# Two attentions on one core: the order of units and projections, VD in six instructions, score heads chosen, zero matmuls

## The chip, the cores and the metric

The kernel runs on one core of a Trainium2 chip. The metric is device time in microseconds, the median of three runs. The profile comes from one execution.

## The reference

Two attention layers with 32 heads of 16 on 2048 rows of width 512, their outputs side by side. A works in four segments of 512 rows with a causal mask, and mixes in a memory that the segments before have built up. B is plain full attention.

```python
# A, per segment s (L = 512 rows), M and z start at 0
logits = einsum('bhqd,bhkd->bhqk', qs, ks) * scale + mask
a_dot  = einsum('bhqk,bhkd->bhqd', softmax(logits), vs)
a_mem  = einsum(phi(qs), M) / (einsum(phi(qs), z) + 1e-06)
o      = g * a_mem + (1.0 - g) * a_dot
M, z   = M + einsum(phi(ks), vs), z + phi(ks).sum(rows)
# B
o = einsum(softmax(q @ k.T * Dh**-0.5), v)
# both: o @ wo; result concat([A, B], -1)
```

## The kernel before

**Units.** The work is cut into 64 units, each of four heads and 512 query rows: 32 of A (segment, head group) and 32 of B (query chunk, head group). The four heads sit in the four 32-row groups of the PE array. A bank is one head, 128 keys by 512 queries: a score matmul, an exponential, and a matmul with V into the one accumulator `acc`, in which each head has a 32-column group. A B unit has 64 banks.

**Two engines take exponentials.** ACT reads tiles of three banks and of two (`s0`, `s1`) with one instruction (`act_tile_a`, L639 and L636; `act_tile_b`, L694) and writes `pT`. For A, POOL then sets the part above the diagonal to zero (`affine_select`, L650). Up to 19 banks of a B unit, its list `dl`, go to DVE instead (`dve_bank`): one instruction turns a score bank into integers that are the bits of a float16 power of two (L732), and two cheap ones add a constant (L711, two banks at a time), so that three terms with three scaled copies of V make the exponential. These copies are `VD`, made on POOL for each B unit by `make_vd` (L571) and kept in two buffers. The first B unit has no DVE banks.

**Jobs.** Projections, transposes of x, the memory's steps and the output matmuls ("chores" in the code, jobs here) each fill a bank of `d_ps`, of which there are two, shared with the DVE banks, and DVE empties it. A Q projection is followed by two mask multiplications on POOL (L317) before its unit may start. `setup_late` is a set of some 50 small POOL instructions and the loads of the two output weights.

**Order.** Nothing is scheduled at run time. While the program is built, a planner keeps a clock for each engine, with costs (`act_cost`, `dve_cost`, `gp_do`, `pe`), and in a loop takes the next thing that its clocks allow: an ACT tile of the unit `ai`, a due job, a DVE bank, a new VD, or a batch of matmuls into `acc` for the unit `pvi`. Each engine then runs its own list in that order. Units stand in the order of `useq`: A's first segment, then B and A in turns until A is used up, then the last eight B units alone. A job has a due time counted in units (`due`) and is taken once `prog`, the planner's place, has passed it, or when ACT has nothing that it can start (`stalled`). When a unit is complete, `finalize` transposes `acc` (L761), takes the reciprocal of its sums, scales on POOL (L782 to L785) and transposes back (L789); a chunk's four outputs follow as jobs (L476, L481).

**The end.** After the last unit come its four outputs, and a range check over all sums (L985 to L1001) that decides whether a general path has to run.

Of the kernel before, what the change touches and what calls it, by code (L numbers as in the profile page):

```python
# [41 lines left out]
def fast_path(ctx, tc, nc, A_x, A_wq, A_wk, A_wv, A_wo, A_beta, B_x, B_wqkv, B_wo, out, flag):  # L42
# [77 lines left out]
    mbds = [const.tile([P, HG, 4, 32], BF16, name=f"mbd{i}") for i in range(2)]  # L120
    maskg = const.tile([P, HG, 4, 17], F32, name="maskg")
# [51 lines left out]
    E1 = [(12, 2), (13, 3), (14, 0)]  # L173
    useq = []
    a_rest = [("a", s, hg) for s in range(1, NSEG) for hg in range(HG)]
    b_all = [("b", qc, hg) for qc in range(4) for hg in range(HG)]
    useq += [("a", 0, hg) for hg in range(HG)]
    while b_all:
        useq.append(b_all.pop(0))
        if a_rest:  # L180
            useq.append(a_rest.pop(0))
    def u_left(u):
        if u["k"] == "a":
            return len(u["F"]) + 0.5 * len(u["half"])
        return sum(len(x) for x in u["al"]) + len(u["dl"])

    U = []
    for i, (k, c, hg) in enumerate(useq):
# [5 lines left out]
        else:  # L194
            u["dl"] = [(kb, kb % 4, kb) for kb in range(NSB)] + [(kb, j, kb + 4) for kb, j in E1]
# [5 lines left out]
        u["size"] = u_left(u)  # L201
        U.append(u)
# [18 lines left out]

    def pe(ns, mode, key=None):
# [7 lines left out]
        c["t"] = max(c["t"], ses["base"] + ses["acc"][key])  # L230

    def act_cost(n):
        return 80.0 + 0.833 * n

    def dve_cost(n, rate=1.04):
        return 75.0 + rate * n
# [230 lines left out]
    aT_at = [0.0]  # L467
    OT_t = {}
    tN_t = {}

    def chore_out(k, cc, sbl):
        def fill(bank):
            wo = wo_a if k == "a" else wo_b
            for rt in range(4):
                lhsT = OT_t[(k, cc, rt)][:, 4 * (sbl % 2):4 * (sbl % 2) + 4, :, sbl // 2].rearrange("p c r -> p (c r)")
                nc.tensor.matmul(bank[:], lhsT, wo[:, rt, :], start=(rt == 0), stop=(rt == 3))  # L476
            pe(4 * MM, "full")
# [11 lines left out]

    chores = []  # L490
    now = lambda: c["t"]

    def chore(due, need, fn, ok=None):
# [11 lines left out]
    b0 = uidx[("b", 0, 0)]  # L505
    for i in range(4):
        chore(-9, 0, lambda i=i: chore_v("a", i))
    for rt in range(1, 4):
        chore(2 * rt - 1.7, 2 * rt, lambda rt=rt: chore_k("a", 0, rt))
        chore(2 * rt - 1.6, 2 * rt, lambda rt=rt: chore_q("a", 0, rt))  # L510
    chore(0.5, 2, setup_late)
    for g in range(4):
        for i in (0, 2):
            chore(g, b0 + g / 4, lambda i=4 * g + i: chore_xT("b", i))
        chore(g, b0 + g / 4, lambda g=g: chore_k("b", g, 0))
        if g == 0:
            chore(g, b0, lambda: chore_q("b", 0, 0))
        for i in range(4):
            chore(g, b0 + g / 4 + i / 16, lambda i=4 * g + i: chore_v("b", i))
    for rt in range(1, 4):  # L520
        n = uidx[("b", 0, 2 * rt)]
        for g in range(4):
            chore(n - 3.5 + g / 2, n, lambda g=g, rt=rt: chore_k("b", g, rt))
        chore(n - 1.5, n, lambda rt=rt: chore_q("b", 0, rt))
    for qc in range(1, 4):
        for rt in range(4):
            n = uidx[("b", qc, 2 * rt)]
            chore(n - 2.5, n, lambda qc=qc, rt=rt: chore_q("b", qc, rt), ok=lambda qc=qc, rt=rt: q_free("b", qc, rt))
    for s in range(1, NSEG):
        n = uidx[("a", s, 0)]  # L530
        f = 1.0 if s > 1 else 0.5
        for i in range(4):
            chore(n - f * (8 - 0.7 * i), n, lambda s=s, i=i: chore_kphi(s - 1, i),
                  ok=lambda s=s, i=i: (kphi_n.get(s - 1, 0) == i and phik_at.get((s - 1, i - 2), 0 if i < 2 else 1e18) <= now()
                                       and len(v_ready) >= NSB + 4))
        for half in range(2):
            chore(n - f * (5 - 0.4 * half), n, lambda s=s, half=half: chore_macc(s - 1, half),
                  ok=lambda s=s: phik_n.get(s - 1) == 4 and phik_at[(s - 1, 3)] <= now())
        for i in (0, 2):
            chore(n - f * (4.2 - 0.2 * i), n, lambda s=s, i=i: chore_xT("a", 4 * s + i),  # L540
                  ok=lambda s=s: xT_uses.get(("a", s - 1), 0) == (14 if s == 1 else 16))
        chore(n - f * 3.7, n, lambda s=s: seg_v(s))
        for i in range(4):
            chore(n - f * (3.6 - 0.5 * i), n, lambda s=s, i=i: chore_v("a", 4 * s + i),
# [854 lines left out]
```

## Time and profile before

| what | value |
|---|---|
| median of three runs | 1141.72 us (1133.79 to 1144.57) |
| profiled execution | 1138.61 us, span 1136.8 us |
| PE busy, share of the span | 916.4 us, 81% |
| ACT busy | 855.8 us, 75% |
| DVE busy | 789.7 us, 69% |
| POOL busy | 492.8 us, 43% |
| mean granted PE clock | 0.827 |

Lines such as L694 are those of the kernel before. "Idle before" is how long the engine stood still ahead of an instruction, and the arrow names what ended it. PEclk is the granted clock, 1.00 at full speed. PE's busy time counts matmuls whose ends are modelled, and four matmuls in four row or column groups overlap.

### The profile page before, as it was taken

Reading aid. Unit: us, or ns where it says so; the run is one execution under the profiler, and the core shown is the slowest. Engines: PE = TensorE matmul, PEld = TensorE weight load, DVE = VectorE, ACT = ScalarE, POOL = GpSimd, SP = SyncE. Lnnn points to the kernel's source line nnn. Section 1 sums busy time; section 2 is a strip of 40 time slices with the busy share of each in tenths; the row PEclk is TensorE's granted clock in tenths of the full one; section 3 lists DMA queues with packets and bytes.
Section 4 is the critical chain, followed back from the end, with each engine's and each line's share of the span. In section 5 each row is a group of like instructions: output and inputs, shape, how many; then the busy total and the mean of one; then the engine's idle time right before and its main releaser. Section 6 shows DMA issues by size and latency. Waiting matters only on the chain.

```text
span 1136.8 us, 18722 instructions
## 1 busy us (share of the span) xinstructions
PE 916.4 (81%) x6979; PEld 256.9 (23%) x7012; DVE 789.7 (69%) x1559; ACT 855.8 (75%) x781; POOL 492.8 (43%) x1343
## 2 busy tenths in 40 slices
PE   6786988787978887787788788887888798887883
PEld 2332221222212221222222221221222221222111
DVE  3452567877767757787878857787768666778675
ACT  4334898986877486888888888797878877789772
POOL 2749234455534734645452535545453402233200
PEclk8896997889666898888989996797769986689678
DMA  5200000000000010000000010000000000000000
GB/s 160 79 26 19 19 1 1 1 1 11 5 1 2 1 36 4 1 1 1 1 1 2 1 38 1 1 1 1 1 1 1 15 25 1 1 1 1 2 1 22
DMA packets 13956, 13.87 MB, mean 12 GB/s; under 512 B 2336, under 2 KB 13600, under 8 KB 13856
## 3 DMA queue, kind: packets, MB, share of 16 engines
q1 hardware_dynamic: 12096, 10.75, 2.9%
q8 instruction: 56, 0.92, 0.3%
q0 software_dynamic: 416, 1.05, 0.3%
q10 hardware_dynamic: 1344, 0.79, 0.2%
q14 instruction: 44, 0.36, 0.1%
HBM read 8.39 MB, written 4.19 MB: 11 GB/s over the span
## 4 chain that ended last, share of the span: by engine, by line
PE 38%; ACT 24%; POOL 14%; issue 13%; DVE 9%; DMA 1%; ACTq 0%; DVEq 0%; POOLq 0%
ACT pT L694 20%; PE acc L823 16%; PE s_ps L689 9%; POOL VD L571 7%; ACT pT L639 4%; PE d_ps L721 3%; DVE pD L732 3%; PE d_ps L304 3%; DVE pD L711 2%; PE d_ps L307 2%; PE s_ps L629 2%; DVE tT L761 2%; POOL pT L650 1%; PE d_ps L476 1%; DMA beta_t<-in_A_beta_dram 1%
## 5 line engine op out<-in xcount | busy, mean ns | idle before, releaser
L694 ACT ACTIVATE pT<-s_ps 128x1536 bf16<-128x1536 f32 (+1 forms) x593 | 689.1, 1262 | 171.5 <-PE s_ps L689 140.8
L732 DVE TENSOR_SCALAR pD<-d_ps 128x512 int16<-128x512 f32 x566 | 377.5, 682 | 161.3 <-PE d_ps L721 148.8
L689 PE MATMUL s_ps<-QT_b,KT_b 32*128 32x512 bf16 x1482 | 263.0, 449 | 106.6 <-ACT pT L694 98.7
L823 PE MATMUL acc<-pD,VD 128*32 128x512 f16 x1698 | 306.2, 469 | 5.0 <-DVE pD L711 2.7
L823 PE MATMUL acc<-pT,VP_b 128*32 128x512 bf16 x1482 | 283.2, 468 | 9.4 <-DVE tT L761 8.0
L650 POOL TENSOR_SCALAR_AFFINE_SELECT pT<-pT 128x512 bf16<-128x512 bf16 (+3 forms) x192 | 95.9, 516 | 333.0 <-ACT pT L639 331.5
L721 PE MATMUL d_ps<-QT_b,KT_b 32*128 32x512 bf16 x566 | 228.0, 443 | 9.1 <-DVE pD L732 4.7
L711 DVE TENSOR_SCALAR pD<-pD 128x1024 int16<-128x1024 int16 x566 | 234.9, 456 | 0.2
L571 POOL TENSOR_SCALAR VD<-VP_b 128x72 bf16<-128x72 bf16 (+1 forms) x744 | 186.4, 251 | 47.8
L639 ACT ACTIVATE pT<-s_ps 128x1280 bf16<-128x1280 f32 (+1 forms) x128 | 137.8, 1173 | 54.0 <-PE s_ps L629 52.3
L689 PEld LDWEIGHTS <-KT_b 32*128 32x128 bf16 x1482 | 65.9, 94 | 365.0 <-issue 362.2
L823 PEld LDWEIGHTS <-VD 128*32 128x32 bf16 x1698 | 68.1, 103 | 106.8 <-issue 94.1
L823 PEld LDWEIGHTS <-VP_b 128*32 128x32 bf16 x1482 | 64.3, 104 | 116.2 <-issue 103.7
L629 PE MATMUL s_ps<-QT_a,KT_a 32*128 32x512 bf16 (+3 forms) x512 | 62.8, 331 | 22.1 <-ACT pT L639 10.7
L782 POOL TENSOR_TENSOR tN<-tT,RA 128x256 bf16<-128x256 f32 x31 | 20.4, 660 | 132.4 <-DVE RA L764 132.4
L823 PE MATMUL acc<-pT,VP_a 128*32 128x384 bf16 (+3 forms) x512 | 35.7, 332 | 35.4 <-POOL pT L650 23.7
L761 DVE STREAM_TRANSPOSE tT<-acc 128x512 f32<-128x512 f32 x64 | 45.4, 710 | 25.2 <-PE acc L823 24.7
L721 PEld LDWEIGHTS <-KT_b 32*128 32x128 bf16 x566 | 49.4, 96 | 16.3 <-issue 16.0
L317 POOL TENSOR_SCALAR QT_b<-qc,mq 128x512 bf16<-128x512 bf16 x32 | 22.9, 726 | 45.9 <-DVE qc L375 45.6
L481 DVE CAST osb<-d_ps 128x512 bf16<-128x512 f32 x32 | 22.0, 690 | 28.6 <-PE d_ps L476 25.4
L629 PEld LDWEIGHTS <-KT_a 32*128 32x128 bf16 x512 | 20.3, 94 | 86.4 <-issue 81.2
L823 PEld LDWEIGHTS <-VP_a 128*32 128x32 bf16 x512 | 14.3, 99 | 61.9 <-issue 38.8
(107 smaller groups left out, 613.5 us busy)
## 6 DMA issues: line engine op xcount, KB each, us to landing
out_dram<-osb SPq DMA_DIRECT2D x32, 128.0 KB, 1.7
xin<-in_B_x_dram SPq DMA_DIRECT2D x16, 128.0 KB, 2.3
xin<-in_A_x_dram SPq DMA_DIRECT2D x14, 128.0 KB, 2.3
wv_a<-in_A_wv_dram SPq DMA_DIRECT2D x1, 512.0 KB, 10.4
wv_b<-in_B_wqkv_dram SPq DMA_DIRECT2D x1, 512.0 KB, 12.2
wk_b<-in_B_wqkv_dram SPq DMA_DIRECT2D x1, 512.0 KB, 11.8
wq_b<-in_B_wqkv_dram SPq DMA_DIRECT2D x1, 512.0 KB, 11.5
wo_a<-in_A_wo_dram POOLq DMA_DIRECT2D x1, 512.0 KB, 4.8
```

The costliest lines, as they stand in the source:

```text
L304: nc.tensor.matmul(bank.rearrange("p (n s) -> p n s", n=4), w[:, cc, wsl], xt[:, :, cc, :], start=(cc == 0), stop=(cc == 3))
L571: mul = lambda dst, src: nc.gpsimd.tensor_scalar(dst, src, EXP_C[k], 1.0, ALU.mult, ALU.mult)
L629: nc.tensor.matmul(pt[:, b, col:col + w], kt[32 * j:32 * j + 32, kbl * P:(kbl + 1) * P], q[32 * j:32 * j + 32, P * kbl:512], start=(r == 0 ...
L639: nc.scalar.activation(pT[:].rearrange("p b n -> p (b n)")[:, 0:n], pt[:].rearrange("p b n -> p (b n)")[:, 0:n], ACT.Exp, scale=0.25)
L650: nc.gpsimd.affine_select(out=blk, in_=blk, compare_op=ALU.is_ge, fill=0.0, base=0, pattern=[[0, e - b], [0, w // P], [1, P]], channel_mul ...
L689: nc.tensor.matmul(pt[:, b, :], KT_b[32 * j:32 * j + 32, u["rt"], kb * P:(kb + 1) * P], q[32 * j:32 * j + 32, :], start=True, stop=True, t ...
L694: nc.scalar.activation(pT[:, 0:n, :], pt[:, 0:n, :], ACT.Exp, scale=1.0 / (LOG2E * 1024.0))
L711: nc.vector.tensor_scalar(tile[:, k, 0:n, :], tile[:, 0, 0:n, :], EXP_D[k], None, ALU.add)
L721: nc.tensor.matmul(bank[:], KT_b[32 * j:32 * j + 32, u["rt"], kb * P:(kb + 1) * P], qslice(u)[32 * j:32 * j + 32, :], start=True, stop=Tru ...
L732: nc.vector.tensor_scalar(pd[:, 0, n, :], bank[:], EXP_B, 0.0, ALU.add, ALU.max)
L761: nc.vector.transpose(tT[:].rearrange("p c d -> p (c d)"), u["acc"][:])
L823: nc.tensor.matmul(u["acc"][32 * j:32 * j + 32, e["c0"]:512], e["lhsT"], e["rhs"], start=(j not in u["started"]), stop=False, tile_positio ...
```

## The change

- **Units**: after A's first segment come two B units, then the other 24 A units spread evenly among B's 30 that follow, so that a B unit is the last.
- **Jobs**: due times are now in nanoseconds of planned progress, set shortly before the unit that needs them, and then pushed ahead from the last to the first, so that neighbours are at least 1200 ns apart near the start and 2500 ns later.
- **VD**: one multiplication for the 16 blocks and one for the 3 extra ones, for each of three terms: 6 instructions of 288 and 54 elements a unit instead of 24 of 72 and 18.
- **Heads**: DVE banks of a unit are taken in any order of heads. One beside an ACT tile takes a head that the tile leaves free; it also waits for its keys in the plan.
- **Zero matmuls**: where the planner sees PE idle for over 300 ns and the last window of 3413 ns poorly filled, it adds matmuls with a zero operand to `acc`. 16 are in the built program.
- **End**: 12 of the last chunk's 16 output matmuls stand ahead of the last unit's end, in the banks of ACT's tiles; two of its four evacuations and output loads go to ACT's queue. The range check has two instructions fewer.
- **Planner's costs**: ACT 100 instead of 80 ns fixed, DVE 1.09 and 0.32 instead of 1.04 and 0.26 ns an element. As a result 554 banks go to DVE instead of 566, and ACT takes 12 more.

```diff
+    zero = const.tile([P, P], BF16, name="zero")
+    nc.vector.memset(zero[:], 0.0)
...
-    E1 = [(12, 2), (13, 3), (14, 0)]
-    while b_all:
-        useq.append(b_all.pop(0))
-        if a_rest:
-            useq.append(a_rest.pop(0))
+    E1 = [(13, 0), (14, 1), (15, 2)]
+    useq = [("a", 0, hg) for hg in range(HG)]
+    for n in range(4 * HG):
+        useq.append(("b", n // HG, n % HG))
+        while a_rest and 30 * (24 - len(a_rest)) < 24 * (n - 1):
             useq.append(a_rest.pop(0))
...
+        u["est"] = 5300.0 if k == "a" else 1200.0 + 463.0 * sum(len(x) for x in u["al"])
+        u["at"] = U[-1]["at"] + U[-1]["est"] if U else 10000.0
...
-            chore(g, b0 + g / 4, lambda i=4 * g + i: chore_xT("b", i))
+            chore(n - 5500, lambda i=4 * g + i: chore_xT("b", i))
...
+    chores.sort(key=lambda x: (x["need"], x["n"]))
+    n = 1e18
+    for x in chores[::-1]:
+        n = x["due"] = min(x["need"], n - (1200 if x["need"] < b0 + 35000 else 2500))
...
         for k in range(NT):
             mul = lambda dst, src: nc.gpsimd.tensor_scalar(dst, src, EXP_C[k], 1.0, ALU.mult, ALU.mult)
-            for r in range(4):
-                mul(t[:, k, 0:NSB * VW]...[:, :, r, :], vb[:, :, r * ROW + o + 2 * VW * r:...])
-            for r in range(4):
-                mul(t[:, k, (NSB + r) * VW:(NSB + r + 1) * VW], VP_b[:, 12 + r, ...])
+            mul(t[:, k, 0:NSB * VW]..., heads_of(0, [[4 * ROW, 4], [step, 4]]))
+            mul(t[:, k, NSB * VW:(NSB + len(E1)) * VW]..., second)
...
+    def dve_head(u, but=()):
+        left = [sum(1 for e in u["dl"] if e[1] == j and has_keys(u, e[0])) for j in range(4)]
+        js = [j for j in range(4) if left[j] and j not in but]
+        return max(js, key=lambda j: (left[j], -j)) if js else None
...
+    def fill_idle(until):
+        u = U[pvi[0]]
+        n = 0
+        while until - c["t"] > 300 and n < 8 and busy(until - 3413) < 3100:
...
+                nc.tensor.matmul(u["acc"][:], zero[:], wq_a[:, 0, :], start=False, stop=False, skip_group_check=True)
...
+    def tail_open():
+        tail["banks"] = []
...
+        for sbl in range(4):
+            for rt in range(3):
+                out_mm(tail["banks"][sbl], "b", 3, sbl, rt, rt == 0, False)
```

What this does to the order of instructions is shown at three places. First DVE near the start, between the transposes that end A units 1 and 2. VP_b, KT_b and xT_b are B's values, keys and transposed x, KT_a and qc the next A projections. Before:

```order
L761 STREAM_TRANSPOSE tT<-acc 128x512
L764 RECIPROCAL RA<-tT 128x16
L389 CAST VP_b<-d_ps 128x32x16 x2
L789 STREAM_TRANSPOSE OT<-tN 128x256
L389 CAST VP_b<-d_ps 128x32x16
L349 CAST KT_a<-d_ps 128x512
L373 CAST qc<-d_ps 128x512
L294 COPY xT_b<-d_ps 128x1024 x2
L349 CAST KT_b<-d_ps 128x512
L389 CAST VP_b<-d_ps 128x32x16 x4
L294 COPY xT_b<-d_ps 128x1024
L761 STREAM_TRANSPOSE tT<-acc 128x512
```

And now, at the same place:

```order
L808 STREAM_TRANSPOSE tT<-acc 128x512
L811 RECIPROCAL RA<-tT 128x16
L361 CAST KT_a<-d_ps 128x512
L306 COPY xT_b<-d_ps 128x1024
L836 STREAM_TRANSPOSE OT<-tN 128x256
L306 COPY xT_b<-d_ps 128x1024
L808 STREAM_TRANSPOSE tT<-acc 128x512
```

Thirteen jobs of d_ps lay between the two transposes of acc; now there are three, and most of B's values follow later.

Second POOL, where VD is made for the first time. Before, two units' VD stand between the causal masks (AFFINE_SELECT) of A's units; the first of them and its neighbours:

```order
L650 AFFINE_SELECT pT_823<-pT_823 128x2x128
L571 TENSOR_SCALAR VD<-VP_b 128x4x18 x4
L571 TENSOR_SCALAR VD<-VP_b 128x18 x4
L571 TENSOR_SCALAR VD<-VP_b 128x4x18 x4
L571 TENSOR_SCALAR VD<-VP_b 128x18 x4
L571 TENSOR_SCALAR VD<-VP_b 128x4x18 x4
L571 TENSOR_SCALAR VD<-VP_b 128x18 x4
L578 MEMSET VD 128x3x14
```

And now, behind all masks of A's first segment and the Q masks of B's second head pair:

```order
L825 TENSOR_SCALAR rw<-RA,omg 128x16
L829 TENSOR_TENSOR tN<-tT,rw 128x8x2x16
L329 TENSOR_SCALAR QT_b<-qc,mq 128x512 x2
L605 TENSOR_SCALAR VD<-VP_b 128x288
L605 TENSOR_SCALAR VD<-VP_b 128x54
L605 TENSOR_SCALAR VD<-VP_b 128x288
L605 TENSOR_SCALAR VD<-VP_b 128x54
L605 TENSOR_SCALAR VD<-VP_b 128x288
L605 TENSOR_SCALAR VD<-VP_b 128x54
L608 MEMSET VD 128x3x14
```

24 multiplications have become 6, and they no longer stand ahead of a mask that A's first segment waits for.

Third DVE again, where A's last segment is prepared. In the new program this stands in one stretch without a DVE score bank (pD from d_ps) between:

```order
L306 COPY xT_a<-d_ps 128x1024 x2
L496 CAST osb<-d_ps 128x512
L401 CAST VP_a<-d_ps 128x32x16 x2
L496 CAST osb<-d_ps 128x512
L385 CAST qc<-d_ps 128x512
L401 CAST VP_a<-d_ps 128x32x16
L361 CAST KT_a<-d_ps 128x512
L401 CAST VP_a<-d_ps 128x32x16
L387 TENSOR_SCALAR qc<-d_ps 128x512
L385 CAST qc<-d_ps 128x512
L361 CAST KT_a<-d_ps 128x512
L387 TENSOR_SCALAR qc<-d_ps 128x512
```

Two more jobs follow in it. In the old program the jobs for A's last segment are spread, as its second and third block of values:

```order
L732 TENSOR_SCALAR pD<-d_ps 128x512
L389 CAST VP_a<-d_ps 128x32x16 x2
L761 STREAM_TRANSPOSE tT<-acc 128x512
L764 RECIPROCAL RA<-tT 128x16
L454 STREAM_TRANSPOSE aT<-d_ps 128x512
L457 TENSOR_SCALAR r_7327<-aT 128x16
L458 RECIPROCAL r_7327<-r_7327 128x16
L732 TENSOR_SCALAR pD<-d_ps 128x512
```

Sixteen jobs of d_ps now follow each other between two ACT tiles, where DVE's score banks and the jobs stood in turns.

More of the change, by code (lines that the diff above doesn't have):

```diff
@@ L220, in d_done, with busy @@
         dcount[0] += 1
+    work = []
+    def busy(since):
+        while work and work[0][0] < since:
+            work.pop(0)
+        return sum(w for _, w in work)
     def pe(ns, mode, key=None):
@@ L560, in fast_path @@
     VD_t, VD_at = {}, {}
-    NSL = NSB + 4
+    NSL = NSB + len(E1)
     def make_vd(u):
@@ L661, in act_tile_a @@
                                      v=("a", 4 * u["c"] + kbl)))
+        return [j for j, _ in banks]
     def nbanks(u):
```

220 lines of the change are left out of this document (135 added, 85 removed).

## The prediction, made before the changed kernel ran

> **What bounds the kernel now.** I read the slices first, then the busy time of three stages, then the waits and the chain.
>
> ```profile
> ACT  4334898986877486888888888797878877789772
> PEclk8896997889666898888989996797769986689678
> core 0: us, PE busy (x) PEld busy (x) DVE busy (x) ACT busy (x) POOL busy (x), PEclk, DMA share, GB/s
> 0.00:110.00 110.00, 77.21 (x488) 29.84 (x496) 43.84 (x89) 43.89 (x49) 64.53 (x190) 0.81 0.24 73
> 110.00:1117.00 1007.00, 834.85 (x6474) 225.54 (x6500) 736.63 (x1453) 811.90 (x733) 427.92 (x1153) 0.83 0.02 5
> 1117.00:1137.00 20.00, 4.35 (x27) 1.50 (x18) 9.24 (x18) 0.00 (x0) 0.38 (x1) 0.73 0.09 31
> PE 38%; ACT 24%; POOL 14%; issue 13%; DVE 9%; DMA 1%; ACTq 0%; DVEq 0%; POOLq 0%
> ACT pT L694 20%; PE acc L823 16%; PE s_ps L689 9%; POOL VD L571 7%; ACT pT L639 4%; PE d_ps L721 3%; DVE pD L732 3%; PE d_ps L304 3%; DVE pD L711 2%; PE d_ps L307 2%; PE s_ps L629 2%; DVE tT L761 2%; POOL pT L650 1%; PE d_ps L476 1%; DMA beta_t<-in_A_beta_dram 1%
> DVE pD L732 <- PE d_ps L721: 148.8, 217, 2.3
> ACT pT L694 <- PE s_ps L689: 140.8, 101, 8.4
> PE s_ps L689 <- ACT pT L694: 98.7, 186, 2.6
> ```
>
> Three stages differ. In the first 110 us ScalarE (ACT), which does most of the exponentials, works 43.9 us, 40%. In the next 1007 us it works 811.9, 80.6%, with VectorE (DVE) at 73%. The last 20 us hold no ACT work. In the middle nothing is full: ACT and DVE wait for TensorE (PE), and PE waits for ACT, in turns. So time is to be had in two ways: start the middle earlier, or take stalls out of it.
>
> PE's speed is part of this. Four neighbouring stretches of 3.4 us:
>
> ```profile
> 1043.89:1047.30 3.41, 2.45 (x39) 0.75 (x31) 2.65 (x5) 2.39 (x3) 2.74 (x10) 1.00 0.00 0
> 1047.30:1050.72 3.42, 2.33 (x28) 0.55 (x22) 2.46 (x5) 3.42 (x4) 2.76 (x11) 1.00 0.00 0
> 1050.72:1054.13 3.41, 3.41 (x23) 0.67 (x16) 2.08 (x5) 2.43 (x3) 1.61 (x7) 0.57 0.00 0
> 1054.13:1057.54 3.41, 3.41 (x21) 0.70 (x24) 2.21 (x6) 2.99 (x3) 0.00 (x0) 0.50 0.02 5
> ```
>
> The granted clock goes from 1.00 to 0.50 and ACT from 3.42 us of work to 2.43 and 2.99. A mean of 0.83 over the middle means about a third of it at half clock.
>
> **The start.** B's first unit opens after eight A units. ACT's timeline, cut to the ends of the waits, one row of PE's, and one stretch of the busy times (columns as above):
>
> ```profile
> 28.49 0.62 ACT L636 ACTIVATE pT<-s_ps 128x512 bf16<-128x512 f32 x1
> 40.44 4.20 ACT L639 ACTIVATE pT<-s_ps 128x1280 bf16<-128x1280 f32 x4 [11.34 <-PE s_ps L629]
> 52.67 2.15 ACT L639 ACTIVATE pT<-s_ps 128x1280 bf16<-128x1280 f32 x2 [6.44 <-PE s_ps L629]
> 56.33 0.60 ACT L636 ACTIVATE pT<-s_ps 128x512 bf16<-128x512 f32 x1
> 70.01 4.20 ACT L639 ACTIVATE pT<-s_ps 128x1280 bf16<-128x1280 f32 x4 [13.08 <-PE s_ps L629]
> 79.85 0.59 ACT L636 ACTIVATE pT<-s_ps 128x512 bf16<-128x512 f32 x1
> 95.61 4.20 ACT L639 ACTIVATE pT<-s_ps 128x1280 bf16<-128x1280 f32 x4 [12.35 <-PE s_ps L629]
> 109.68 1.45 ACT L694 ACTIVATE pT<-s_ps 128x1536 bf16<-128x1536 f32 x1
> 71.63 1.04 PE L307 MATMUL d_ps<-wv_b,xT_b 128*128 128x512 bf16 x4
> 83.66:90.69 7.03, 0.00 (x0) 0.00 (x0) 0.00 (x0) 0.00 (x0) 5.59 (x24) 0.61 0.00 0
> ```
>
> ACT sees the pairs of A units start at 40.4, 70.0 and 95.6, with waits of 11.3, 13.1 and 12.4 us ahead of them. The first two are runs of projections on PE (11 and 10 d-bank jobs between two ACT tiles, counted in the built order); the third is GpSimd (POOL) making two VD tiles while every other engine stands still (row 83.66). The change scatters the jobs, one behind a tile, and makes VD after B has begun. The wait of 6.4 us stays, because setup_late still stands in front of the masks of units 2 and 3. So I lay the pairs end to end: first pair done at 29.1 (28.49 + 0.62), second pair 16.5 us (40.4 to 56.9, its wait kept), two more at 10.4 (70.0 to 80.4, a pair with jobs between its tiles) to 14.1 us (95.6 to 109.7). B opens at 66 to 74; I take 70.5, **39 us earlier**.
>
> That is not all gain. Of the jobs that stood ahead of B's first tile 17 now follow it (9 V, 2 K, 2 transposes, 4 for the memory), each 1.04 us of PE. If they hide beside ACT they cost 0, if not 18. PE was busy 77 of those 110 us, and 835 of the next 1007, so I take half: +9. The start is worth **-30** (-39 to -21). What else these jobs issue has room where it goes: their DVE evacuations (0.67 each) fall beside B's first unit, which has no DVE banks; the transposes' x loads and the outputs between them on SP's queue meet a DMA share of 0.02; the memory's POOL steps (three a job) come while POOL is busy 42%.
>
> **Clumps in the middle.** The old order has two more runs of 8 jobs between two ACT tiles; the new has one of 7 and one of 16, when A's last segment is prepared (third order excerpt).
>
> ```profile
> 269.80:281.10 11.30, 8.62 (x59) 3.52 (x59) 10.14 (x18) 2.48 (x6) 9.32 (x17) 1.00 0.08 25
> 376.50:394.50 18.00, 14.63 (x77) 4.69 (x76) 13.77 (x22) 4.72 (x7) 16.45 (x25) 0.85 0.00 1
> ```
>
> In these two ACT idles 8.8 and 13.3 us, 22.1 for 16 jobs: 1.38 each. 23 jobs cost 31.7: **+9** (0 if ACT has tiles left to chew, +10 if not).
>
> **VD on POOL.** 24 multiplications for each of 31 units become 6.
>
> ```profile
> L571 POOL TENSOR_SCALAR VD<-VP_b 128x72 bf16<-128x72 bf16 x372 | 98.8, 265 | 24.3
> L571 POOL TENSOR_SCALAR VD<-VP_b 128x18 bf16<-128x18 bf16 x372 | 87.6, 236 | 23.5
> L317 POOL TENSOR_SCALAR QT_b<-qc,mq 128x512 bf16<-128x512 bf16 x32 | 22.9, 726 | 45.9 <-DVE qc L375 45.6
> sum 228.97, PE 175.63 PEld 45.22 DVE 151.09 ACT 182.91 POOL 184.25; mean PE 5.32 PEld 1.37 DVE 4.58 ACT 5.54 POOL 5.58
> DVE OT L789 <- POOL tN L785: 19.8, 8, 4.1
> PE acc L823 <- POOL pT L650: 9.0, 5, 3.5
> ```
>
> The fourth row sums the stretches in which VD is made (31 units, asked for in 33 pieces): 229.0 us, 7.4 a unit, of it 184.3 busy, so 0.06 us of gap at each of 744. From 18 to 72 elements an instruction grows by 0.030 us, 0.00056 an element; from 18 to QT_b's 512 it is (0.716 - 0.236)/494 = 0.00097. So 288 elements take 0.39 to 0.50, 54 take 0.26 to 0.27, and a unit 2.3 to 2.7 with gaps: 4.7 to 5.1 less. The chain gives VD 7% of the span, 80 us, or 13 units at 5.94 us busy; 2 are in the start, already counted. The other 11 bound the gain at 11 x 4.9 = 54. The other end is nothing: ACT worked 182.9 of these 229 us, 80%, as much as in the rest of the middle. Between them lie the waits for POOL's late work in the middle: 19.8 for DVE, 9.0 for PE (last two rows). I take 20 of these 28.8, since some lie side by side: **-20**. What is late next is ACT's own work and PE's clock.
>
> **Heads.** A DVE score bank now takes a row group of the array that the ACT tile beside it leaves free.
>
> ```profile
> 1112.15 0.39 PE L689 MATMUL s_ps<-QT_b,KT_b 32*128 32x512 bf16 x3 [0.20 <-ACT pT L694]
> 1112.37 0.37 PE L721 MATMUL d_ps<-QT_b,KT_b 32*128 32x512 bf16 x1
> ```
>
> Here the fourth matmul starts 0.22 us after the three that go together: one serial round. Counted over both built orders (longest row group of each run, in 512 columns), score rounds fall from 890 to 802.5, while rounds into acc rise from 1100.75 to 1121.5 and full ones from 628.75 to 644.75, the latter the 16 zero matmuls. Net -67 without those, 15 us at 0.22, 29 at half clock. PE holds 38% of the chain: **-6** (-11 to 0, since there are 78 more changes of tile shape).
>
> **Banks.** 12 banks move from DVE to ACT.
>
> ```profile
> L694 ACT ACTIVATE pT<-s_ps 128x1536 bf16<-128x1536 f32 x297 | 438.4, 1476 | 95.1 <-PE s_ps L689 85.1 <-PE d_ps L721 8.9
> L732 DVE TENSOR_SCALAR pD<-d_ps 128x512 int16<-128x512 f32 x566 | 377.5, 682 | 161.3 <-PE d_ps L721 148.8 <-PE s_ps L689 9.6
> L711 DVE TENSOR_SCALAR pD<-pD 128x1024 int16<-128x1024 int16 x566 | 234.9, 456 | 0.2
> ```
>
> ACT gains 12 x 0.492 = 5.9 us, DVE loses 12 x (0.667 + 0.415) = 13.0. **0**, between +6 and -13: neither is full.
>
> **Zero matmuls.** 16 in all, in 11 places: 3.5 us at 0.22, 7 at half clock if nothing hides them; if each place saved one stretch from half clock (ACT 3.42 against a mean of 2.71 in the rows above, 0.7), -8. **0**. The trace bears on why they are there: 1047.30 has 28 matmuls, no gap near its own length, and the clock falls right behind it. The Trainium skill (TensorE: Matmul & The Clock Gate, section "HAM oscillation — how this bites in real kernels") states the rule as "no PE-idle gaps >~3.4µs". By that rule the zeros would bring nothing in the middle and the sum would be 3.5 to 7 higher; the trace differs, since the clock halves with PE 2.33 of 3.42 us busy.
>
> **The end.** 12 of the last 16 output matmuls move ahead of the last unit's end, and two of four evacuations go to ACT.
>
> ```profile
> 1119.82 3.06 PE L476 MATMUL d_ps<-wo_b,OT 128*128 128x512 bf16 x13 [1.37 <-DVE OT L789]
> 1123.65 0.69 DVE L481 CAST osb<-d_ps 128x512 bf16<-128x512 f32 x1 [0.16 <-DMA out_dram<-osb]
> ```
>
> From 1119.8 to 1124.3 becomes 4 matmuls and two evacuations, some 2: **-2.5** (0 to -3).
>
> **Sum.** -30 + 9 - 20 - 6 + 0 + 0 - 2.5 = -49.5. The profiled run took 1138.6 us (span 1136.8), so 1089; the median shown is 3.1 above it, so **1092**.
>
> **Rivals.** (1) *POOL was the pacemaker*: VD gives its full 54 instead of 20, and the steadier flow of matmuls keeps the clock up; 1092 - 34 = 1058, lower still if half-clock time shrinks. For it: 7% of the chain. Against: ACT at 80% while VD is made. (2) *The gain is taken back*: all 17 moved jobs cost the 1.38 of a clump (+23), VD and heads nothing, banks +6, zeros +7, the clump +10: -39 + 23 + 6 + 7 + 10 - 2.5 = +4.5, 1146; with half of these prices 1119. For it: PE is busy 83% of the middle and every engine waits for another in turn. (3) *Late projections become the wait*, the side that is slower. In 13 places of the later segments and chunks a Q projection now stands 5 to 18 ACT tiles before its first use; before, none after the start stood nearer than 18. Its way is 1.04 on PE, 0.67 on DVE and 2 x 0.72 for the masks on POOL, 3.2 us; five tiles last 6.3 (1.26 a tile). It decides once POOL's queue (a VD of 2.5, causal masks) makes each come over 49.5/13 = 3.8 us late; at 7 us it is 1092 + 91 = 1183. (4) *It does not do what it says*: only 16 zeros are placed, so the clock stays as it was; that is in the forecast.
>
> **How the numbers follow.** Forecast (1074 to 1110) 0.55; rival 1 (below 1074) 0.22; rival 2 (1110 to 1150) 0.16; rival 3 (above) 0.07. The range, 1050 to 1130, takes in most of rival 1 and the near half of rival 2. 1% is about what a measurement of this kernel can tell from no change; under 1130 counts as faster: 0.85, within 0.08, slower 0.07.
>
> **What would show it.** B's first L722 tile on ACT near 70 us; no stretch like 83.66; VD stretches of 2.5 us and VD nearly gone from the chain; an ACT hole of some 20 us before A's last segment; a last output evacuation 2 to 3 us earlier after the last transpose. ACT's share of the middle should rise from 80.6% to 82 or 83; if it stays, the VD term was wrong, and if it falls, look at waits on QT and KT. A much higher granted clock would mean that I undervalued matmul density.

## The result, and the profile after

| what | before | after |
|---|---|---|
| median on the same chip | 1137.99 us | 1023.52 us (1015.13 to 1026.30) |
| ratio, 95% interval | | 0.898 (0.890 to 0.905) |
| profiled execution, span | 1138.61, 1136.8 us | 1026.3, 1024.5 us |
| mean granted PE clock | 0.827 | 0.912 |

The median before is over four runs here; the 1141.72 that the forecast started from is over three of them. Ratios leave out executions more than 1.5% above the fastest of their kernel and medians do not, so the two can differ a little, and the profiles of run 2 and of the old heads in run 5 are of such executions, 7 to 9 us above their medians.

The kernel is 114 us faster. The forecast was 1092 with a range of 1050 to 1130: the sign was right, the size less than half, and the time lies below the range. The profile of after, first its slices for ACT and the clock, then the busy times of the three stages (first 70 us, middle, end), then the chain by engine and line:

```profile
ACT  3489998989989598898988899897489689999791
PEclk9799999998999898998999999899799969989697
core 0: us, PE busy (x) PEld busy (x) DVE busy (x) ACT busy (x) POOL busy (x), PEclk, DMA share, GB/s
0.00:70.00 70.00, 49.62 (x361) 18.25 (x361) 27.14 (x65) 37.75 (x40) 43.14 (x121) 0.90 0.29 93
70.00:1005.00 935.00, 759.42 (x6624) 230.87 (x6623) 747.51 (x1453) 817.03 (x748) 331.51 (x664) 0.92 0.02 7
1005.00:1024.50 19.50, 3.61 (x23) 1.14 (x21) 8.04 (x16) 1.17 (x2) 0.38 (x1) 0.65 0.13 41
PE 35%; ACT 34%; issue 17%; DVE 7%; POOL 5%; DMA 1%; ACTq 0%; DVEq 0%
ACT pT L727 30%; PE acc L870 13%; PE s_ps L722 7%; PE d_ps L316 4%; ACT pT L670 4%; PE d_ps L319 3%; DVE pD L779 2%; DVE pD L745 2%; PE s_ps L660 2%; PE d_ps L486 2%; PE d_ps L768 1%; POOL pT L681 1%; POOL VD L605 1%; DMA wk_a<-in_A_wk_dram 1%; DVE tT L808 1%
```

The first stage is 40 us shorter (110 to 70). The middle is 72 us shorter (1007 to 935) with 5 us more work on ACT (811.9 to 817.0): its idle time there fell from 195 to 118 us, and its share rose from 80.6% to 87.4%, where I had 82 to 83. PE's busy time in it fell by 75 us. POOL fell in the chain from 14% to 5%, VD from 7% to 1%. So the start came as forecast, and what I missed lies in the middle. Waits of the whole execution (total, times, longest), and below them one row of the kernel before that has not been shown yet:

```profile
DVE pD L779 <- PE d_ps L768: 95.2, 182, 1.7
ACT pT L727 <- PE s_ps L722: 34.7, 31, 7.4
ACT pT L727 <- PE d_ps L768: 55.8, 54, 5.6
PE s_ps L722 <- ACT pT L727: 121.5, 237, 1.4
```

```profile
ACT pT L694 <- PE d_ps L721: 26.4, 36, 2.3
```

DVE waits 95.2 us for its score banks where it waited 148.8; ACT waits 34.7 for its own score matmuls where it waited 140.8, and 55.8 for a DVE bank's matmul that PE has just ahead, where it waited 26.4; PE waits for ACT longer than before (121.5, 98.7). The balance has shifted: the longest row was DVE's wait for PE, now it is PE's wait for ACT. ACT and DVE together still wait longer for PE (185.7 us in the three rows) than PE does for ACT.

### The profile page after: what moved, and what is told of

Its sections match the earlier page's. It is cut to its first block, busy times and chain, and to the rows that moved or that the text cites. A ratio compares the mean times of both kernels' runs of the same rounds, so it can differ in the third digit from the quotient of the medians.

```text
span 1024.5 us, 18143 instructions
## 1 busy us (share of the span) xinstructions
PE 812.7 (79%) x7004; PEld 250.3 (24%) x7004; DVE 782.7 (76%) x1532; ACT 855.9 (84%) x790; POOL 375.0 (37%) x785
## 4 chain that ended last, share of the span: by engine, by line
PE 35%; ACT 34%; issue 17%; DVE 7%; POOL 5%; DMA 1%; ACTq 0%; DVEq 0%
ACT pT L727 30%; PE acc L870 13%; PE s_ps L722 7%; PE d_ps L316 4%; ACT pT L670 4%; PE d_ps L319 3%; DVE pD L779 2%; DVE pD L745 2%; PE s_ps L660 2%; PE d_ps L486 2%; PE d_ps L768 1%; POOL pT L681 1%; POOL VD L605 1%; DMA wk_a<-in_A_wk_dram 1%; DVE tT L808 1%
## 5 line engine op out<-in xcount | busy, mean ns | idle before, releaser
L727 ACT ACTIVATE pT<-s_ps 128x1536 bf16<-128x1536 f32 (+1 forms) x600 | 690.3, 1265 | 93.5 <-PE d_ps L768 55.8
L779 DVE TENSOR_SCALAR pD<-d_ps 128x512 int16<-128x512 f32 x554 | 370.5, 682 | 103.1 <-PE d_ps L768 95.2
L722 PE MATMUL s_ps<-QT_b,KT_b 32*128 32x512 bf16 x1494 | 242.8, 410 | 129.1 <-ACT pT L727 121.5
L870 PE MATMUL acc<-pT,VP_b 128*32 128x512 bf16 x1494 | 274.0, 424 | 1.7 <-DVE tT L808 1.7
L870 PE MATMUL acc<-pD,VD 128*32 128x512 f16 x1662 | 267.3, 425 | 3.6 <-DVE tT L808 2.1
L768 PE MATMUL d_ps<-QT_b,KT_b 32*128 32x512 bf16 x554 | 215.7, 413 | 3.2 <-DVE pD L779 2.1
L870 PEld LDWEIGHTS <-VD 128*32 128x32 bf16 x1662 | 61.4, 99 | 85.9 <-issue 74.3
L660 PE MATMUL s_ps<-QT_a,KT_a 32*128 32x256 bf16 (+3 forms) x512 | 59.4, 318 | 28.5 <-ACT pT L727 13.0
L605 POOL TENSOR_SCALAR VD<-VP_b 128x288 bf16<-128x288 bf16 (+1 forms) x186 | 66.8, 359 | 12.3
L870 PE MATMUL acc<-pT,VP_a 128*32 128x256 bf16 (+3 forms) x512 | 36.9, 317 | 19.6 <-POOL pT L681 11.3
L329 POOL TENSOR_SCALAR QT_a<-qc,mq 128x512 bf16<-128x512 bf16 x30 | 21.8, 738 | 54.2 <-DVE qc L385 54.1
## 6 DMA issues: line engine op xcount, KB each, us to landing
wq_b<-in_B_wqkv_dram SPq DMA_DIRECT2D x1, 512.0 KB, 10.4
```

Source lines behind the costliest of these rows:

```text
L329: nc.gpsimd.tensor_scalar(t[:, par, :], qc[:], mq[:, par:par + 1], 1.0, ALU.mult, ALU.mult)
L605: mul = lambda dst, src: nc.gpsimd.tensor_scalar(dst, src, EXP_C[k], 1.0, ALU.mult, ALU.mult)
L660: nc.tensor.matmul(pt[:, b, col:col + w], kt[32 * j:32 * j + 32, kbl * P:(kbl + 1) * P], q[32 * j:32 * j + 32, P * kbl:512], start=(r == 0 ...
L722: nc.tensor.matmul(pt[:, b, :], KT_b[32 * j:32 * j + 32, u["rt"], kb * P:(kb + 1) * P], q[32 * j:32 * j + 32, :], start=True, stop=True, t ...
L727: nc.scalar.activation(pT[:, 0:n, :], pt[:, 0:n, :], ACT.Exp, scale=1.0 / (LOG2E * 1024.0))
L768: nc.tensor.matmul(bank[:], KT_b[32 * j:32 * j + 32, u["rt"], kb * P:(kb + 1) * P], qslice(u)[32 * j:32 * j + 32, :], start=True, stop=Tru ...
```

## The experiments

Each run changes one thing, or two, in the kernel after or before. They ran in five groups, each beside the kernel before on the same chip, so I compare ratios; "worth n us" is a difference of ratios times 1138. A difference between two kernels other than the one before is good to about 11 us (8 to 15).

**1. VD's multiplications as before, in the new order.**

```diff
-            mul(t[:, k, 0:NSB * VW]..., heads_of(0, [[4 * ROW, 4], [step, 4]]))
-            mul(t[:, k, NSB * VW:(NSB + len(E1)) * VW]..., second)
+            for r in range(4): mul(one of the four 72-element parts)
+            for r in (0, 1, 2, 2): mul(one block of 18)
```

> The changed kernel with VD made in 24 multiplications a unit again (the 16 blocks in four of 72 elements, the extra ones in four of 18, one of them twice), and every other instruction in the same order. Theory P (POOL's VD was the pacemaker of the middle): most of the 76 us that the middle lost come back, 1075 to 1100 us, granted clock 0.83 to 0.87, VD on the chain again with 5% or more. Theory H (score heads in free row groups) and theory J (jobs spread out): at most 15 us come back, the clock stays above 0.90. My forecast of -20 for this part says 1043.

1102.28 us, ratio 0.972 (0.967 to 0.978): worth 85 us, nearly three quarters of the 116 that the ratio of after makes. That is theory P, a little above its 1075 to 1100. The plan in this run still counts 1.8 us for a VD; run 3 takes that up. The waits in it, and the same rows of after:

```profile
PE acc L873 <- POOL pT L684: 56.7, 16, 8.7
DVE tT L811 <- PE acc L873: 48.0, 12, 7.3
DVE OT L839 <- POOL tN L835: 11.7, 3, 4.4
```

```profile
PE acc L870 <- POOL pT L681: 11.3, 7, 8.7
DVE tT L808 <- PE acc L870: 5.7, 6, 2.3
DVE OT L836 <- POOL tN L832: 0.3, 1, 0.3
```

A VD of 7.4 us stands on POOL in front of causal masks. PE stands still at acc matmuls that need a masked tile (56.7 against 11.3 us), and DVE behind it waits with the transposes that end a unit (48.0 against 5.7). 57 us of direct waits for masks and tN went with 85 by the ratios, and with 76 between the two profiled spans (1100.3 and 1024.5).

**2. The same in the old order.** 9 instructions (288, 36 and 36 elements for each term) in place of 24, nothing else.

> The kernel before in its own order, with only VD's multiplications shortened: 9 a unit (288, 36 and 36 elements) instead of 24, the same blocks, the same order on every other engine. Its stretch on POOL falls from 7.4 us to some 3.0 (3 x 0.45 + 6 x 0.25 busy and 9 gaps of 0.06). Theory W (POOL's work itself was the price, in any order): it gains as much as the new order lost with the old VD, 79 us, so 1055 to 1070, and the granted clock rises to 0.87 or more. Theory N (the price is one of the new order, whose masks stand close behind a VD): it gains 15 to 35 us as my forecast had it, 1100 to 1120, with the clock near 0.84.

1102.93 us, ratio 0.961 (0.950 to 0.971): worth 45 us (33 to 57), between the theories. B's first tile comes at 99.2 instead of 109.7, so some 10 of it are the start and 35 the middle. So the price of POOL's work depends on the order that stands around it.

**3. Only the plan told the truth.** Here not one instruction is removed; the order, and in the new kernel some banks and zero matmuls, follow anew from the price. Before, and after with the old multiplications:

```diff
-            gp_do(36, max(v_ready.values()))      # before, 24 times a unit: 3.3 us
+            gp_do(198, max(v_ready.values()))     # 7.4 us
-            gp_do(100, 0)                         # after, 3 times a unit: 1.8 us in all
+            gp_do(1872, 0)                        # 7.4 us
```

> The kernel before, with nothing changed but that the planner is told 7.4 us for a unit's VD where it assumed 3.3 (24 instructions at 308 ns instead of 138). Theory M: it gains 30 us or more, below 1105, with the 24 multiplications still there. Theory W: within 12 us of the kernel before, 1122 to 1147. Its order also has 21 more score rounds and 12 more rounds into acc, 7 us at 0.22, which both theories take off the gain.

> The changed kernel with the 24 old multiplications, as in the run at 1102 us, but with the planner told what they take (7.4 us a unit instead of 1.8), so that the order leaves room for them. Theory M (the plan is what fails: it places matmuls before POOL can have made their masks, and PE takes its list in order): most of the 79 us comes back, 1025 to 1060, and PE's wait for causal masks falls from 57 us towards 11. Theory W (POOL's work costs wherever it stands): 1085 to 1105.

1100.96 us, ratio 0.966 (0.959 to 0.973), and 1069.07, 0.941 (0.934 to 0.948). Telling the planner what VD takes was worth 39 us in the old order, with the 24 multiplications in place, and 35 of the 85 in the new one. The first is theory M; the second lies between M (1025 to 1060) and W (1085 to 1105). What is left of the 85, 50, is the work itself or the other order that the truth brings (56 zero matmuls in it for 16, 562 banks on DVE for 554). The rows of the kernel before, of the old order told, of run 2, and of the new order with old multiplications told:

```profile
PE acc L823 <- POOL pT L650: 23.7, 10, 9.2
```

```profile
PE acc L823 <- POOL pT L650: 25.9, 8, 9.2
DVE OT L789 <- POOL tN L785: 2.3, 2, 1.6
```

```profile
PE acc L826 <- POOL pT L653: 7.4, 6, 3.5
DVE OT L792 <- POOL tN L785: 0.9, 1, 0.9
```

```profile
PE acc L873 <- POOL pT L684: 24.4, 11, 8.7
DVE tT L811 <- PE acc L873: 26.2, 10, 6.5
DVE OT L839 <- POOL tN L835: 2.7, 3, 1.6
```

In the old order, telling the plan took away DVE's wait for tN (19.8 to 2.3), not PE's for masks. In the new order it took away both in good part: masks 56.7 to 24.4, tN 11.7 to 2.7, together 41 us, as much as the profiled span got shorter (1100.3 to 1058.7). Shortening VD took both away in the old order too; with the new heads in that order (run 5) the masks' row fell from 37.5 to 8.9 by it. Of the 39 us in the old order these rows explain 18 at most; ACT's wait for its score matmuls fell beside them (140.8 to 106.9), and how the two hang together isn't shown. Any new price also gives a new order. That alone could be worth something, but the other new orders of the kernel after (runs 4 and 9) moved the time by 6 us at most.

Run 2 makes the price true as well: its VD takes about the 3.3 us that the old plan counts (3.43 us at 169.47 on POOL, 3.17 at 228.08). So of its 45 us only some 6, less than the error, are left for the shorter work itself; in the new order it is the 50.

**4. The changed kernel told the truth too** (2.5 us; `gp_do(316, 0)`).

> The changed kernel with the planner told 2.5 us for a unit's VD, which is what its trace shows (2.44 us from the first multiplication to the end of the memset's predecessor), where it assumes 1.8. Theory M (wherever the plan is too short for POOL, PE is sent to wait): the same or some us faster, 1010 to 1026, since the error is now 0.7 us a unit instead of 5.6 in the run with the old multiplications. The clump of 16 jobs stays (15). Theory W gives no reason for a change: within 5 us.

1026.71 us, 0.901 (0.899 to 0.904): no difference that can be told. An error of 0.7 us a unit costs nothing that can be told; one of 4 to 5.6 cost 35 to 39.

**5. The old heads in the new order; the new heads in the old order, with and without the short VD.** DVE's banks in the list's order, and the ACT tile not told of them:

```diff
-        left = [sum(1 for e in u["dl"] if e[1] == j and has_keys(u, e[0])) for j in range(4)]
-        js = [j for j in range(4) if left[j] and j not in but]
-        return max(js, key=lambda j: (left[j], -j)) if js else None
+        return next((e[1] for e in u["dl"] if has_keys(u, e[0])), None)
```

> The changed kernel, planned anew with DVE's banks taken in their fixed order and no head kept free beside an ACT tile; serial score rounds go from 802 back to 908, 10 more banks go from DVE to ACT. Theory H: 30 us or more slower, DVE's waits for its score banks (L768) from 95 back towards 149 us, clock lower. Theories P and J: within 12 us of 1023 (106 rounds less 40 acc rounds, at 0.22 us and PE's third of the chain, are 5).

> The kernel before with the free choice of heads alone (24 multiplications for VD, old order of units and jobs): 84 score rounds fewer, 7 into acc more, 13 more banks on DVE. By full price of a round (theory F) 77 x 0.22 / 0.84 = 20, and 13 banks less on ACT, 6.4: 15 to 30 us faster, 1105 to 1125. If the 38 us that the heads gave beside the short VD were there only because POOL was out of the way, it is less than 10 us.

> The kernel before with the shorter VD and with the free choice of heads, still its old order of units, its old due times and its old costs. 13 more banks go to DVE (579), score rounds fall from 890 to 806. If the heads are worth here what taking them away cost in the new order (26 us), it lies 20 to 30 us below the kernel with the short VD alone; by my forecast 5 to 10. With the short VD at 79 (theory W) that makes 1030 to 1045, with the short VD at 25 (theory N) 1080 to 1105.

Old heads in the new order: 1049.50, 0.924 (0.917 to 0.931), worth 30. New heads alone in the old order: 1110.89, 0.978 (0.973 to 0.984), worth 25 (19 to 31). Beside the short VD: 1064.89, 0.934 (0.928 to 0.941), another 30. So heads are worth 25 to 30 in each of the three places, and add up with VD. The change of heads brings one of banks with it: the new heads put 13 banks more on DVE in the old order and the old heads 10 fewer in the new one, 5 to 6 us of ACT's work at 0.492 each, so a part of the 25 to 30 may be that. The waits of the old heads, and of the new heads in the old order:

```profile
DVE pD L777 <- PE d_ps L766: 132.6, 202, 2.2
ACT pT L727 <- PE s_ps L722: 101.7, 77, 9.9
ACT pT L727 <- PE d_ps L766: 19.1, 25, 3.3
```

```profile
DVE pD L745 <- PE d_ps L734: 96.8, 176, 2.2
ACT pT L694 <- PE s_ps L689: 77.4, 41, 9.7
ACT pT L694 <- PE d_ps L734: 54.4, 52, 4.2
```

Against 95.2, 34.7 and 55.8 after, and 148.8, 140.8 and 26.4 before: with the new heads DVE waits less for its score banks and ACT less for its own score matmuls. ACT waits more for a DVE bank's matmul just ahead of them, so its two rows together fall by 35 us in the old order and by 30 in the new one.

**6. What a round on PE costs.** Behind every fourth, or every, batch of acc matmuls four with a zero operand, one for each column group:

```diff
+        if len(u["started"]) == 4 and tax[0] % 4 < 1:
+            for j in range(4):
+                nc.tensor.matmul(u["acc"][32 * j:32 * j + 32, :], zero[:, 0:32], wq_a[:, 0, :],
+                                 start=False, stop=False, tile_position=(0, 32 * j), ...)
```

> The changed kernel in its own order, with 424 matmuls with a zero operand added to acc: behind every fourth batch of acc matmuls one for each of the four column groups, so 106 rounds more, all in the tile shape that PE is in at that place, planned by nobody. That is as many rounds as the old heads had more in their score matmuls (908 against 802.5). At 0.22 us and a granted clock of 0.9 it is 25 us of PE's time. Theory F (a round on PE costs its full time, since PE is in nearly every chain of waits): 20 to 30 us slower, 1045 to 1057, which would also explain the 26 us of the heads. Theory S (my forecast, PE's share of the chain, 35 to 38%): 7 to 12 us slower. Theory D (denser matmuls keep the clock up and pay for themselves): within 5 us, with a granted clock above 0.92.

> The changed kernel with the four zero matmuls behind every batch of acc, 427 rounds instead of 106: 93 us of PE's time at 0.218 each, with PE busy 79% of the span before. Theory D says that the clock can pay for at most what it has left: from 0.91 to 1.00, 9% of PE's 813 us, 70 us; so 10 to 45 us slower than the changed kernel, 1035 to 1070, with a clock of 0.97 or more. If PE simply has slack (its rounds hide beside ACT), the time stays within 10 us and the clock need not rise. Theory F: 85 to 95 us slower.

> The kernel before in its own order, with 404 matmuls with a zero operand added to acc: behind every fourth batch one for each column group, 101 rounds, 22 us of PE's time at full clock and 27 at its mean clock of 0.83. In the changed kernel 106 such rounds were free and the granted clock rose from 0.91 to 0.94. Theory D (the clock follows how densely matmuls are started, and sets the time where PE is behind): the clock rises by 0.03 or more from 0.83 and the time falls by 5 to 30 us, 1105 to 1132. Theory F (PE's time is on the path here, where POOL holds it up): 20 to 30 us slower with an unchanged clock, 1155 to 1168. In between (within 5 us of before), the clock pays for the rounds and no more.

> The changed kernel with the old fixed order of heads (1049 us in its run) and with zero matmuls behind every fourth batch (398 more, 100 rounds). Theory D (the old heads cost time since the fourth matmul runs alone, fewer are started in a stretch, and the clock halves oftener): part of the 26 us comes back, 1030 to 1043, with a clock above 0.91. Theory B (the old heads cost by the wait of the DVE bank for its own serial round, whatever the clock): the clock rises but the time stays at 1045 to 1060.

106 rounds in the kernel after: 1023.58, 0.901 (0.898 to 0.903). 427 rounds: 1023.20, 0.898 (0.891 to 0.904). 101 in the kernel before: 1140.33, 0.994 (0.986 to 1.002). 100 beside the old heads: 1074.86, 0.941 (0.930 to 0.952), 19 us (4 to 34) slower than those without. PE's own rows, of the runs with 106 and 427 rounds and of the new heads in the old order:

```profile
PE 808.0 (80%) x7390; PEld 257.8 (25%) x7428; DVE 785.8 (77%) x1532; ACT 854.3 (84%) x790; POOL 374.3 (37%) x785
```

```profile
PE 848.9 (83%) x8673; PEld 284.0 (28%) x8712; DVE 782.8 (77%) x1532; ACT 856.9 (84%) x790; POOL 373.1 (37%) x785
```

```profile
PE 843.2 (76%) x7005; PEld 257.2 (23%) x7038; DVE 797.6 (72%) x1586; ACT 844.4 (76%) x776; POOL 492.7 (44%) x1343
```

| kernel | PE busy, us | granted clock | product |
|---|---|---|---|
| before | 916.4 | 0.827 | 758 |
| new heads in the old order | 843.2 | 0.882 | 744 |
| after | 812.7 | 0.912 | 741 |
| after, 106 rounds more | 808.0 | 0.944 | 763 |
| after, 427 rounds more | 848.9 | 0.974 | 827 |

The product moves as the counted rounds do: 22 for 106 x 0.218 = 23, 86 for 93, -14 for 77 fewer (17); 0.218 is the planner's price of a round, and the rows of 1112.15 in the prediction have 0.22. (The ends of matmuls are modelled, so the product is an estimate of PE's work.) In these profiles the clock rose with the number of matmuls added. So 106 rounds added no busy time on PE at all, and of 427 the clock paid 58 us (827 / 0.912 - 849); the other 36 hid beside ACT. Theory F is refuted for the kernel after. Theory D's time and clock came for 106 rounds, but not the 10 to 45 us that it had for 427: there the clock came, and the time is that of slack on PE. So these runs don't show that the rise of the clock is what kept the time, since rounds that fit into PE's idle time would give the same. In the kernel before, 101 rounds raised the clock (0.827 to 0.868) and bought nothing that can be told. Beside the old heads neither theory came: D had 1030 to 1043 with a clock above 0.91, B 1045 to 1060 with a raised clock, and the run took 1074.86 at 0.886 in its profile. There the rounds cost about their full price, 22 us at 0.22. Why they are dear there and free in the kernel after stays open: PE was busy 83% of the span with the old heads and rounds, but also with the 427 rounds that cost nothing.

**7. Zero matmuls left out** (the 16 in `fill_idle`, same order).

> The changed kernel with its 16 zero matmuls left out, every other instruction planned as with them. Theory Z (they hold the clock up): clock 0.02 or more lower and 10 to 20 us slower. All others: within 7 us of 1023, the clock within 0.01.

1025.69, 0.904 (0.898 to 0.910): nothing that can be told.

**8. Old due times.** Jobs due by units and without spacing; B opens at 98.95 instead of 73.90.

> The changed kernel with the old due times of jobs, counted in units, without a set spacing; units still in the new order, VD, heads, zeros and end as changed. 44 jobs stand ahead of B's first tile again (26 in the changed kernel), in clumps of 11 and 10, and clumps of 15 and 14 stand in the middle. Theory J (late, spread jobs made the gain): 45 us or more slower, B opens at 95 to 105 us instead of 74. Theories P and H: B opens later by some 22 us (two clumps of 11 and 13 us), and the rest of the middle holds, so 1045 to 1055 with a clock of 0.90 or more in the middle.

1037.71, 0.918 (0.911 to 0.925): worth 23 us for 25 us of start, with a range of 11 to 34, which fits theories P and H.

**9. Units in turns, DVE banks beside B's tiles only, the old costs.** The first two edits are shown; for the third, three numbers go back:

```diff
-        while a_rest and 30 * (24 - len(a_rest)) < 24 * (n - 1):
+        if a_rest and n >= 2:
...
-                js = act_tile_a(act_now)
+                act_tile_a(act_now)
+                continue
```

> The changed kernel with only the list of units changed back to B and A in turns (from the third B unit on) until A is used up, so that the last B units stand alone; all other rules are kept. 15 score rounds fewer, the clump of 16 jobs stands earlier. If spreading A's units over B's is worth something by itself (less ACT per unit of time while A units pass, masks further apart), it is 8 to 20 us slower, 1034 to 1046; if not, within 6 us of the changed kernel.

> The changed kernel without one rule that I had not priced: DVE banks are no longer placed right beside an ACT tile of an A unit, in a head that it leaves free, only beside those of B units as in the kernel before. Beside it the planner now places 562 instead of 554 banks on DVE, 28 instead of 16 zero matmuls, and a clump of 14 jobs near A's second segment. If the rule carries a good part of the 27 us that lie between the kernel with short VD and free heads alone (1065) and the one with the old due times (1038), it is 12 to 25 us slower, 1036 to 1050; if not, within 6 us.

> The changed kernel with the planner's old costs for ACT and DVE (80 ns, 1.04 and 0.26 ns an element), all else as it is. 9 more banks go to DVE (563), 7 score rounds fewer. If the truer costs are worth something (as the truer price of VD was), 8 to 20 us slower, 1032 to 1044; if not, within 6 us.

1025.49, 0.901 (0.898 to 0.904); 1030.02, 0.903 (0.895 to 0.911); 1017.99, 0.894 (0.887 to 0.902). None of the three can be told from the kernel after. With the old costs 563 banks go to DVE, so 9 of the 12 banks that ACT took over follow from the costs.

**10. setup_late four units later**, with 106 rounds (`begin("a", 0, 6)` for `begin("a", 0, 2)`).

> The changed kernel with zero matmuls behind every fourth batch, and setup_late's POOL instructions due four A units later (at the seventh unit instead of the third), so that they no longer stand in front of the masks of units 2 and 3; ACT's wait of 10.6 us ahead of 46.33 should shrink to 3 to 7. If what is gained at the start stays (as it did for half of it when B was opened earlier), 4 to 8 us below the changed kernel with the zero matmuls, 1015 to 1020; if VP_b's preparation is then late for B's first unit, no gain or a few us of loss.

1022.66, 0.898 (0.891 to 0.905): no gain. B's first tile comes at 72.35, and a new wait of 7.2 us for score matmuls stands where 10.6 was. No version that I ran is surely better than the change itself.

## Why the prediction was too small, step by step

**VD: the step that failed.** I put it at -20 (0 to -54), as 20 of the 28.8 us in which DVE and PE wait for POOL's late work. In the old order it was some 35 in the middle; in the order that the kernel now has it was 85, or 50 once the plan knows what a VD takes. Two things were wrong. I took the direct waits for the most that a stall can cost: in the new order 57 us fewer of them went with 76 to 85. And I took the old order's waits as the measure, while the change moves the masks as well. That the planner counted 3.3 us for 7.4 was in reach (the code has one price, the row 229 us for 31 units the other), and I did not set the two beside each other; the runs of 3 show that this alone is worth 35 to 39. My argument for the other end, that ACT was 80% busy while VD was made, was no evidence: the waits that run 1 added are those for masks and tN, which POOL makes later than VD. Rival 1 was the nearest, with 54 and a rising clock; it too was short.

```profile
L605 POOL TENSOR_SCALAR VD<-VP_b 128x288 bf16<-128x288 bf16 (+1 forms) x186 | 66.8, 359 | 12.3
104.55 2.38 POOL L605 TENSOR_SCALAR VD<-VP_b 128x288 bf16<-128x288 bf16 x6
```

The sizes of the instructions were right: a unit takes 2.38 us, within 2.3 to 2.7.

**Heads** were the second: -6 (-11 to 0) against 25 to 30. I multiplied 15 us of rounds by PE's 38% of the chain. The share of one chain is not the price of a stall on an engine that two others wait for: DVE's wait for its banks fell by 52 us in the old order (148.8 to 96.8) and ACT's for PE, both rows together, by 35 (167.2 to 131.8). With the clock that came with it (0.827 to 0.882) PE's busy time is 73 us shorter, of which the rounds themselves are 14 to 17. I had written that a much higher clock would mean that I undervalued matmul density. The clock rose, but run 6 doesn't bear that reading out: added matmuls raised it in the kernels before and after and bought no time.

**Start.** ACT's rows:

```profile
29.54 4.20 ACT L670 ACTIVATE pT<-s_ps 128x1280 bf16<-128x1280 f32 x4 [0.97 <-PE s_ps L660]
46.33 2.15 ACT L670 ACTIVATE pT<-s_ps 128x1280 bf16<-128x1280 f32 x2 [10.56 <-POOL QT_a L329]
73.90 1.45 ACT L727 ACTIVATE pT<-s_ps 128x1536 bf16<-128x1536 f32 x1
```

In the second pair stands the wait that I kept, 10.56 us instead of 6.44, and B opens at 73.9, in my span of 66 to 74 at its late end. -36 instead of -39. With the old due times the time is 23 us longer (11 to 34) for 25 us of start, so most of it stays, as far as that range tells; the +9 for the jobs that moved was not measured by itself.

**Clumps.** The 16 jobs ahead of A's last segment:

```profile
708.30 2.37 ACT L727 ACTIVATE pT<-s_ps 128x1024 bf16<-128x1024 f32 x2 [1.64 <-PE s_ps L722]
715.27 0.63 ACT L371 ACTIVATE eq<-qc 128x512 bf16<-128x512 bf16 x1 [4.61 <-DVE qc L385]
719.75 0.63 ACT L371 ACTIVATE eq<-qc 128x512 bf16<-128x512 bf16 x1 [3.85 <-DVE qc L385]
727.10 1.02 ACT L727 ACTIVATE pT<-s_ps 128x1024 bf16<-128x1024 f32 x1 [6.72 <-PE s_ps L722]
731.34 7.04 ACT L727 ACTIVATE pT<-s_ps 128x1536 bf16<-128x1536 f32 x6 [3.22 <-PE d_ps L768]
```

4.61 + 3.85 + 6.72 + 3.22 = 18.4 us of holes, 20.0 with the 1.64 ahead: right for this clump (16 x 1.38 = 22). What the smaller one of 7 jobs cost is in no row here.

**Zero matmuls** 0: leaving them out made no difference that can be told (7 us, good to 11). Of the rule of the Trainium skill that I weighed (TensorE: Matmul & The Clock Gate, section "HAM oscillation — how this bites in real kernels", no idle gaps on PE over some 3.4 us) these runs show the other side: PE has one gap as long in the kernel after, 8.71 us ahead of 44.36 near the start, and matmuls added behind batches all through the kernel raised the clock from 0.912 to 0.944 and 0.974, and bought no time.

**End.**

```profile
1009.12 0.45 DVE L836 STREAM_TRANSPOSE OT<-tN 128x256 f32<-128x256 f32 x1
1017.24 0.15 DVE L1098 CAST flag<-okc 128x1 int32<-128x1 f32 x1 [0.55 <-POOL okc L1097]
```

From the last transpose to the flag it is 8.3 us, where before it was 10.4 (1119.31 to 1129.68): -2.1 for -2.5. The last output evacuation ends 3.8 us after the start of that transpose (ACT's, 1012.96) where it was 5.0 (1124.34), so 1.2 sooner and not the 2 to 3 that I had as a sign; DVE, which has two fewer of them, starts the shorter range check sooner. Rival 3, late projections, did not come: behind the start, all waits on QT together are under 2 us, and the 8.9 us of ACT's waits on qc are nearly all in the clump above. Rival 2's second time was mis-added: half of its prices is 23, and -39 + 23 - 2.5 from 1142 is 1123, not 1119; nothing hangs on it.

**What stays open.** In ratios the way down is VD in the old order 45, heads 30, the rest 41. Of the rest the due times carry 23 and the end 2; units' order, costs, the banks beside A's tiles and the zero matmuls nothing that one run can tell. Some 16 us, about the error of these differences, have no owner; they may be the same thing as VD's 45 becoming 85, an interaction of order and POOL, which no run shows. Nor was a kernel run in which the clock was held and the heads changed, so how the 25 to 30 of the heads divide between clock, waits and the banks that move with them isn't settled.

## What to carry to other kernels

Where a planner orders the program ahead of time, compare each of its prices with the profile first: here one that was too low by half cost 39 us in the old order, and the shorter work gained 45 there, which made the price true as well. The price of work on an engine off the path is read from what stands behind it in that engine's queue and who waits for that, not from what the others do while it runs. In the table of run 6 PE's busy time is about its work over the granted clock: multiply the two before calling PE full, and test slack by adding matmuls, not by the share of a chain.

## What was not expected of the hardware

427 rounds of zero matmuls, 93 us of work at 0.218, changed the time by nothing (0.898 in both ratios): the granted clock went from 0.912 to 0.974 and PE's busy time only from 812.7 to 848.9 us. The granted clock is not one function of the matmuls started per us either: 7344 in a span of 1068.6 us (old heads with added rounds, 6.9 a us) were granted 0.886, 7004 in 1024.5 (after, 6.8 a us) 0.912. The two differ in how many score matmuls run four abreast; whether that is the reason was not tried.
